# A prologue re-cut: x loaded in parts of 10, 10, 8 and 4, more filler matmuls, and one S2 group issued earlier

## The chip, the cores and the metric

The kernel runs on one core of a Trainium2 chip. The time is the device time of one execution in microseconds; smaller is better. Kernels are compared with runs of the kernel before, or of one another, on the same chip in the same rounds.

Engine names: PE is the matmul engine (PEld its weight loads), DVE the vector engine, ACT the scalar engine, POOL GpSimd, SP the queue that issues the stores. In a profile row the first two numbers are the start and the duration in us, L253 is a line of that kernel, `out<-in` are the program's tiles, xN the number of instructions merged into the row, and the bracket at the end tells how long the engine had been idle and what ended the wait. A "look" is one profiled execution. A part of x has "landed" when its transfer is complete. To "evict" is to copy a finished matmul result out of the matmul engine's output memory (PSUM). A "filler" is a matmul on zeros that nobody reads. "Cold" means that the profile shows half the full clock for PE (0.50 in its clock column; "warm": 1.00). The changed kernel has one line more near the top, so L252, L261, L277, L285, L293, L314 of the kernel before are L253, L262, L278, L286, L294, L315 of the changed one.

## The reference, cut to what matters

```python
X = np.fft.rfft(x, axis=1)                    # x: 8 x 3008 x 256
Y = X * (filt_r + 1j * filt_i)[None]
y = np.fft.irfft(Y, n=3008, axis=1).astype(np.float32)
h = y.reshape(24064, 256) @ w_in              # 256 x 2048
out = np.maximum(0.01 * h, h) @ w_out         # 2048 x 256
```

The Fourier part is done as matmuls: 3008 = 94 x 32 is split into n1 (94) and n2 (32). S1 is the transform over n1 (one matmul for each n2), a transpose on DVE (T1) turns the tile, S2 is the transform over n2, the filter is a product on DVE or POOL, SA and SB are the inverse of S2 and S1 with a transpose (T2) between. Then come the two matmuls of the MoE part with a leaky ReLU between.

## The kernel before

The first batch element cannot hide behind anything, so the kernel has a prologue of its own for it, cut into two halves of the channels (hf). All later elements run inside the slots of the MoE loop. The parts that the change touches:

```python
    for i in range(FP):                       # FP = 4, step = 8 n2
        x_load(0, step * i, step)
    ...
def first_s1(n0, n, kind, copy):              # n matmuls, then one eviction by DVE or ACT
def first_s2(hf, c, n, on_pool):              # n // 4 matmuls, products on DVE, or ACT copies and POOL
def first_sa(hf, c):                          # needs the products; evicted by ACT
def keep_warm(n):                             # n matmuls on zeros that nobody reads
    ...
    keep_warm(28)
    for g in range(6):
        first_s1(4 * g, 4, "ph", (dve, act)[g % 2])
        if g % 2:
            keep_warm(3)
    for g in range(4):
        first_s1(24 + 2 * g, 2, two[g == 3], (act, dve)[g % 2])
    keep_warm(11)
    t1_part(0, 0, True)(), t1_part(0, 1, True)()
    ...
    first_s2(1, 8, 8, True)
    first_sa(0, 8), first_sa(0, 20)
    first_s2(1, 0, 8, False)
    keep_warm(3)
    ...
    first_s2(1, 16, 8, False)
    keep_warm(4)
    first_sa(1, 0)
    keep_warm(4)
    first_t2(0), first_t2(1)
    first_sa(1, 16), first_sa(1, 8)
    first_t2(2), first_t2(3)
```

Of the kernel before, what the change touches and what calls it, by code (L numbers as in the profile page):

```python
# [18 lines left out]
N1, N2 = 94, 32  # L19
# [3 lines left out]
FP = 4  # L23
# [42 lines left out]
def kernel(  # L66
# [50 lines left out]
    def bank(kind, n, w):  # L117
        of = wide if kind == "ph" else single
        t = of[turn[kind] % len(of)]
        turn[kind] += 1  # L120
        return t[:, : n * w].rearrange("p (n w) -> p n w", n=n)
# [7 lines left out]
    def x_load(b, n0=0, nn=N2, d0=0, dn=D):  # L129

        for lo, cnt in ((0, R1),) if b + 1 < B else ((0, 64), (64, N1 - 64)):
            nc.gpsimd.dma_start(  # L132
                x_sb[lo : lo + cnt, ds(n0, nn), ds(d0, dn)],
                bass.AP(tensor=x.tensor, offset=x.offset + (b * N + lo * N2 + n0) * D + d0,
                        ap=[[N2 * D, cnt], [D, nn], [1, dn]]))
# [10 lines left out]
    step = N2 // FP  # L146
    for i in range(FP):
        nc.sync.dma_start(f1_sb[:, ts(i, step), :], f1_d.ap()[i])
    nc.sync.dma_start(small_sb[:], small_d.ap())
    for i in range(FP):  # L150
        x_load(0, step * i, step)
    for hf in range(2):
        filt_load(fa_sb, filt_r, hf * DH, DH)
        filt_load(fb_sb, filt_i, hf * DH, DH)
# [23 lines left out]
    def paired(t):  # L178
        return t[:].rearrange("p (e n t) -> p n e t", n=Q, t=2)

    def spread(dst, n0, ps, copy, e0=0):
        nn, de = ps.shape[1], ps.shape[2] // 2
        copy(paired(dst)[:, ds(n0, nn), ds(e0, de)], ps.rearrange("p n (e t) -> p n e t", t=2))  # L183
# [3 lines left out]
    def t1_part(b, i, flat=False):  # L187
        def go():
            a = big[(4 * b) % 3][:].bitcast(FP32)[:, ts(i, E4 * Q)].rearrange("p (e n) -> p e n", n=Q)
            o = big[(4 * b + 1) % 3][:].bitcast(FP32)  # L190
            if flat:
                o = o[:, ts(i, E4 * Q)].rearrange("p (e n) -> p e n", n=Q)
            else:
                o = o.rearrange("p (n e) -> p e n", n=Q)[:, ts(i, E4), :]
            nc.vector.transpose(o, a)  # L195
        return go
# [49 lines left out]
    two = ("pf", "ph")  # L246
    act, dve = nc.scalar.copy, nc.vector.tensor_copy

    def first_s1(n0, n, kind, copy):
        ps = bank(kind, n, D)  # L250
        for j in range(n):
            nc.tensor.matmul(ps[:, j, :], f1_sb[:N1, n0 + j, :], x_sb[:N1, n0 + j, :],  # L252
                             start=True, stop=True)  # L253
        spread(big[0], n0, ps, copy)


    def first_s2(hf, c, n, on_pool):
        ps = bank("ph", n, DH)
        src = paired(big[1])
        for j in range(0, n, 4):  # L260
            nc.tensor.matmul(ps[:, ds(j, 4), :].rearrange("p n (e t) -> p n e t", t=2), fwd2,  # L261
                             src[:, ds(c + j, 4), ts(hf, DH // 2)], start=True, stop=True)  # L262
        fs = [f[:, ds(c, n), ts(hf, DH)] for f in (fa_sb, fb_sb)]
        if on_pool:
            y = [outp.tile([P, n, DH], FP16, tag="ost", name=f"fy{i}_h{hf}_c{c}") for i in range(2)]
            xs = [scrp.tile([P, 4, DH], FP32, tag=f"p{j // 4 + 1}", name=f"fx_h{hf}_c{c + j}")
                  for j in range(0, n, 4)]
            for j, xf in enumerate(xs):
                act(xf[:], ps[:, ts(j, 4), :])
            for i in range(2):  # L270
                for j, xf in enumerate(xs):
                    nc.gpsimd.tensor_tensor(y[i][:, ts(j, 4), :], xf[:], fs[i][:, ts(j, 4), :], AL.mult)
        else:
            y = [ypp.tile([P, n, DH], FP16, tag=f"yw{i}", bufs=2, name=f"fy{i}_h{hf}_c{c}")
                 for i in range(2)]
            for i in range(2):
                nc.vector.tensor_tensor(y[i][:], ps, fs[i], AL.mult)  # L277
        ys[(hf, c)] = y  # L278

    def first_sa(hf, c):  # L280
        y = ys.pop((hf, c))
        for j in range(0, y[0].shape[1], 4):
            ps = bank("pf", 4, DH)
            for i, m in enumerate((inv2, inv2x)):
                nc.tensor.matmul(ps, m, y[i][:, ds(j, 4), :], start=(i == 0), stop=(i == 1))  # L285
            act(paired(big[2])[:, ds(c + j, 4), ts(hf, DH // 2)],  # L286
                ps.rearrange("p n (t e) -> p n e t", t=2))
# [24 lines left out]
    def keep_warm(n):  # L312
        for _ in range(n):
            nc.tensor.matmul(po_ps.rearrange("p a d -> p (a d)"), idle[:, 0:P], idle[:],  # L314
                             start=True, stop=True)  # L315

    keep_warm(28)
    for g in range(6):
        first_s1(4 * g, 4, "ph", (dve, act)[g % 2])
        if g % 2:  # L320
            keep_warm(3)
    for g in range(4):
        first_s1(24 + 2 * g, 2, two[g == 3], (act, dve)[g % 2])
    keep_warm(11)
    t1_part(0, 0, True)(), t1_part(0, 1, True)()
    upper(0)
    first_s2(0, 8, 8, True)
# [9 lines left out]
    first_sa(0, 0), first_sa(0, 16)  # L337
    keep_warm(3)
    first_s2(1, 8, 8, True)
    first_sa(0, 8), first_sa(0, 20)  # L340
    first_s2(1, 0, 8, False)
    keep_warm(3)
    nc.gpsimd.dma_start(w_out_sb[:], moe_w_out.rearrange("(ct p) d -> p ct d", p=P))
    first_s2(1, 16, 8, False)
# [84 lines left out]
    for slot in range(SL * (NCHUNK + 1)):  # L429
        ci, g = divmod(slot, SL)  # L430
# [36 lines left out]
```

## Time and profile before

| | value | from |
|---|---|---|
| time, median of 3 executions | 785.71 us (785.61 to 785.92) | result |
| span of the profiled one | 784.2 us (its own time was 786.34 us) | page, result |
| first S1 matmul | 9.23 us | timeline of PE |
| last part of x landed | 15.6 us | issue start plus time to landing |
| first T1 transpose | 17.70 us | timeline of DVE |
| first MoE matmul | 43.88 us | timeline of PE |
| from there to the end | 740.3 us | 784.2 - 43.88 |

A change of the prologue can only shift the start of those 740.3 us. The prediction shows the rows of PE and DVE. Here is the chain of waits of the kernel before through the second half (start, us, what):

```profile
29.40 1.07 ACT fx_h_c L269 x2
30.47 1.00 ACT big L286 x2
31.48 0.06 issue
31.53 1.48 DVE fy_h_c L277 x2
33.02 0.79 issue
33.81 2.36 DVE fy_h_c L277 x2
...
36.62 2.15 ACT big L286 x4
```

The chain runs over ACT's copies and evictions up to 31.5 us and then over DVE's products.

### The profile page before, as it was taken

To read this page: it belongs to the slowest core of one execution; us is meant where nothing else is said; L and a number is where in the kernel's file an instruction comes from. 1 tells how busy PE (TensorE), PEld (TensorE's weight loads), DVE (VectorE), ACT (ScalarE), POOL (GpSimd) and SP (SyncE) were. 2 spreads that over 40 slices of the span, in tenths; PEclk is the share of its full clock that TensorE was granted. 3 is DMA by queue.
4 is the path that set the end of the run, shared out by engine and by line. 5 is a ranking of instruction groups with operands and counts; after the bars stand their busy time and mean duration, and the time that the engine had idled before them with its cause. 6 is when DMAs were issued, how large, how long until landed. Compare 5 with 4: busy or idle time off the path is not lost.

```text
span 784.2 us, 13678 instructions
## 1 busy us (share of the span) xinstructions
PE 775.1 (99%) x5844; PEld 531.3 (68%) x5844; DVE 366.2 (47%) x458; ACT 556.0 (71%) x790; POOL 148.9 (19%) x122
## 2 busy tenths in 40 slices
PE   8999999999999999999999999999999999999998
PEld 4366677666776677766777667776677667676666
DVE  4868760874337642477306754088432765200000
ACT  3686769676686767877687776967669776666664
POOL 4863300250003300052001410024000340000000
PEclk9999999999999999999999999999999999999999
DMA  9943101401041101501104101140100101101111
GB/s 187 210 67 79 38 31 40 109 28 42 28 92 57 35 34 36 112 29 42 36 34 108 41 28 41 33 115 28 41 28 34 36 28 41 41 28 41 41 41 55
DMA packets 36252, 43.38 MB, mean 55 GB/s; under 512 B 8130, under 2 KB 34370, under 8 KB 35522
## 3 DMA queue, kind: packets, MB, share of 16 engines
q0 software_dynamic: 10000, 16.99, 12.3%
q1 hardware_dynamic: 26192, 25.53, 9.3%
q8 instruction: 45, 0.74, 0.4%
q14 instruction: 15, 0.12, 0.0%
HBM read 34.10 MB, written 24.64 MB: 75 GB/s over the span
## 4 chain that ended last, share of the span: by engine, by line
PE 92%; ACT 2%; DVE 1%; issue 1%; ACTq 0%
PE po_ps L389 41%; PE ph L375 40%; PE pf L172 3%; PE pf L239 2%; PE pf L227 2%; PE pf L212 2%; PE pf L389 1%; ACT big L183 1%; ACT gt_c L380 1%; DVE fy_h_c L277 0%; ACT big L286 0%; DVE big L293 0%; PE ph L302 0%; ACT ost_c_t L396 0%; PE pf L302 0%
## 5 line engine op out<-in xcount | busy, mean ns | idle before, releaser
L380 ACT ACTIVATE gt_c<-ph 128x1024 f16<-128x1024 f32 x376 | 385.2, 1025 | 194.5 <-PE ph L375 193.5
L375 PE MATMUL ph<-yt,w_in_sb 128*128 128x512 f16 (+7 forms) x1728 | 386.6, 351 | 0.4 <-ACT gt_c L380 0.2
L389 PE MATMUL po_ps<-w_out_sb,gt_c 128*128 128x256 f16 x2944 | 381.4, 272 | 0.6 <-ACT ost_c_t L396 0.6
L389 PEld LDWEIGHTS <-gt_c 128*128 128x128 f16 x3008 | 290.6, 98 | 86.8 <-issue 1.7
L375 PEld LDWEIGHTS <-w_in_sb 128*128 128x128 f16 x1728 | 162.9, 98 | 95.2 <-issue 1.0
L220 POOL TENSOR_TENSOR y_b_g<-p_b_g,p_b_g 128x512 f16<-128x512 f32 x84 | 107.0, 1273 | 225.8 <-DVE p_b_g L218 225.8
L195 DVE STREAM_TRANSPOSE big<-big 128x1024 f32<-128x1024 f32 x32 | 55.9, 1845 | 127.0 <-ACT big L183 126.8
L183 ACT CAST big<-pf 128x512 f16<-128x512 f32 x190 | 108.9, 606 | 0.2 <-PE pf L252 0.2
L242 DVE CAST yt<-pf 128x376 f16<-128x376 f32 x112 | 56.3, 545 | 85.9 <-PE pf L239 85.9
L216 DVE TENSOR_TENSOR p_b_g<-pf,fa_sb 128x512 f32<-128x512 f32 x84 | 58.1, 692 | 38.8 <-PE pf L212 36.3
L396 ACT COPY ost_c_t<-po_ps 128x256 f32<-128x256 f32 x184 | 69.3, 377 | 6.6 <-PE po_ps L389 5.5
L203 DVE STREAM_TRANSPOSE big<-big 128x1024 f32<-128x1024 f32 x28 | 51.1, 1932 | 34.1 <-ACT big L183 34.1
L217 DVE TENSOR_TENSOR p_b_g<-pf,fb_sb 64x512 f32<-64x512 f32 x84 | 58.2, 693 | 1.1
L218 DVE TENSOR_TENSOR p_b_g<-pf,fb_sb 64x512 f32<-64x512 f32 x84 | 57.4, 683 | 1.1
L132 POOL DMA_DIRECT2D x_sb<-in_x_dram x12 | 6.6, 555 | 255.2 <-PE pf L172 254.4
L239 PEld LDWEIGHTS <-big 128*128 128x128 f16 x448 | 25.7, 98 | 13.2
L172 PE MATMUL pf<-x_sb,f_sb 94*128 94x256 f16 x224 | 33.8, 272 | 0.1
L212 PE MATMUL pf<-big,small_sb 128*128 128x512 f16 x84 | 31.8, 379 | 0.0
L227 PE MATMUL pf<-y_b_g,small_sb 128*128 128x512 f16 x84 | 31.8, 379 | 0.0
L239 PE MATMUL pf<-i_sb,big 128*128 128x94 f16 x448 | 28.7, 206 | 0.0
L172 PEld LDWEIGHTS <-f_sb 94*128 94x128 f16 x224 | 21.0, 97 | 9.5 <-issue 1.3
L314 PE MATMUL po_ps<-idle 128*128 128x512 f16 x72 | 20.8, 432 | 1.2 <-DVE one L161 1.2
(46 smaller groups left out, 157.4 us busy)
## 6 DMA issues: line engine op xcount, KB each, us to landing
out_dram<-ost_c_t SPq DMA_DIRECT2D x92, 256.0 KB, 2.1
x_sb<-in_x_dram POOLq DMA_DIRECT2D x6, 1536.0 KB, 10.8
x_sb<-in_x_dram POOLq DMA_DIRECT2D x4, 384.0 KB, 10.4
w_in_sb<-in_moe_w_in_dram POOLq DMA_DIRECT2D x1, 1024.0 KB, 13.0
w_out_sb<-in_moe_w_out_dram POOLq DMA_DIRECT2D x1, 1024.0 KB, 10.2
x_sb<-in_x_dram POOLq DMA_DIRECT2D x1, 1024.0 KB, 8.1
f_sb<-fwd_const SPq DMA_DIRECT2D x4, 192.0 KB, 5.2
fa_sb<-in_filt_r_dram POOLq DMA_DIRECT2D x4, 192.0 KB, 12.4
```

The source lines that it names most:

```text
L172: nc.tensor.matmul(ps[:, j, :], f1_sb[:N1, n2, :], x_sb[:N1, n2, :], start=True, stop=True)
L183: copy(paired(dst)[:, ds(n0, nn), ds(e0, de)], ps.rearrange("p n (e t) -> p n e t", t=2))
L216: nc.vector.tensor_tensor(p1[:], ps, fa, AL.mult)
L217: nc.vector.tensor_tensor(p2[0:64], ps[64:P], fb[64:P], AL.mult)
L218: nc.vector.tensor_tensor(p2[64:P], ps[0:64], fb[0:64], AL.mult)
L220: nc.gpsimd.tensor_tensor(y1[:], p1[:], p2[:], AL.add)
L239: nc.tensor.matmul(ps[:, j, :], src[:, dt, n2, :], i1_sb[:, n2, :], start=True, stop=True)
L242: copy(yv[:, :, ds(4 * h, 4)], ps.rearrange("p c a -> p a c"))
L375: nc.tensor.matmul(ph[:, j, ds(o, ln)], w_in_sb[:, dt, ts(ct, P)], yts[b % 2][:, dt, ds(lo, ln)], start=(dt == 0), stop=(dt == NDT - 1),)
L380: nc.scalar.activation(gts[ci][:, ds(2 * g, 2), :], ph, AF.Lrelu)
L389: nc.tensor.matmul(po, gts[ci][:, ct, ts(tj, P)], w_out_sb[:, ct, :], start=(ct == 0), stop=(ct == NCT - 1))
L396: nc.scalar.copy(ost[:, tj % 2, :], po)
```

## The change

Its intent: less work left after the last x has landed, a warm PE when S2 begins, and no wait of DVE for the second half's first S2 group of its own.

```diff
-    for i in range(FP):
-        x_load(0, step * i, step)
+    first_parts = ((0, 10), (10, 10), (20, 8), (28, 4))
+    for n0, nn in first_parts:
+        x_load(0, n0, nn)
 ...
     keep_warm(28)
-    for g in range(6):
-        first_s1(4 * g, 4, "ph", (dve, act)[g % 2])
-        if g % 2:
-            keep_warm(3)
-    for g in range(4):
-        first_s1(24 + 2 * g, 2, two[g == 3], (act, dve)[g % 2])
-    keep_warm(11)
+    g = 0
+    for n0, nn in first_parts:
+        while nn:
+            n = 2 if nn % 4 or n0 >= N2 - 4 else 4
+            first_s1(n0, n, two[n // 4], (dve, act)[g % 2])
+            n0, nn, g = n0 + n, nn - n, g + 1
+        keep_warm(5 if n0 < N2 else 14)
 ...
     first_s2(1, 8, 8, True)
+    first_s2(1, 0, 8, False)
     first_sa(0, 8), first_sa(0, 20)
-    first_s2(1, 0, 8, False)
     keep_warm(3)
```

## The prediction

> **What bounds the kernel now.** I read the page first, then the chain of waits in order of time, then the timeline of each engine from 8.5 to 46 us, then the busy time by stretches.
>
> ```profile
> PE 775.1 (99%) x5844; PEld 531.3 (68%) x5844; DVE 366.2 (47%) x458; ACT 556.0 (71%) x790; POOL 148.9 (19%) x122
> ...
> PE 92%; ACT 2%; DVE 1%; issue 1%; ACTq 0%
> ...
> 55.00:100.00 45.00, 44.97 (x295) 28.84 (x295) 37.19 (x43) 33.45 (x47) 15.31 (x12) 1.00 0.27 65
> ```
>
> PE is busy 99% of the span, and from 55 us on it is busy without a gap (44.97 of 45.00). The change touches nothing there, so it can only move the moment at which that stretch starts: all that it wins or loses is a shift of the prologue, 44 us of 784 up to the first MoE matmul (43.88 us). The 99% also deceives in the prologue, because the fillers (matmuls on zeros) count as busy.
>
> The prologue, as DVE and PE lived it:
>
> ```profile
> 13.79 1.03 PE L252 MATMUL ph<-x_sb,f_sb 94*128 94x256 f16 x8 [0.37 <-DMA x_sb<-in_x_dram]
> 14.66 0.81 PE L314 MATMUL po_ps<-idle 128*128 128x512 f16 x3
> 15.66 0.82 PE L252 MATMUL pf<-x_sb,f_sb 94*128 94x256 f16 x6 [0.18 <-DMA x_sb<-in_x_dram]
> ...
> 16.53 2.54 PE L314 MATMUL po_ps<-idle 128*128 128x512 f16 x11
> 20.22 1.88 PE L261 MATMUL ph<-big,small_sb 128*128 128x512 f16 x4 [1.14 <-DVE big L195]
> ...
> 28.26 1.02 PE L261 MATMUL ph<-big,small_sb 128*128 128x512 f16 x2
> 29.11 1.47 PE L285 MATMUL pf<-fy_h_c,small_sb 128*128 128x512 f16 x6
> 30.42 1.02 PE L261 MATMUL ph<-big,small_sb 128*128 128x512 f16 x2
> ```
>
> ```profile
> 17.70 2.37 DVE L195 STREAM_TRANSPOSE big<-big 128x1024 f32<-128x1024 f32 x2
> ...
> 22.19 1.23 DVE L277 TENSOR_TENSOR fy_h_c<-ph,fa_sb 128x1024 f16<-128x1024 f32 x1 [1.13 <-PE ph L261]
> ...
> 28.24 1.90 DVE L309 COPY fb_sb<-fb_sb 64x3072 f16<-64x3072 f16 x1
> 31.53 1.22 DVE L277 TENSOR_TENSOR fy_h_c<-ph,fa_sb 128x1024 f16<-128x1024 f32 x1 [1.40 <-ACT big L286]
> ...
> 38.79 2.37 DVE L293 STREAM_TRANSPOSE big<-big 128x1024 f32<-128x1024 f32 x2 [0.36 <-ACT big L286]
> ```
>
> The reader should see four things. Up to 15.66 us PE waits for x, so the end of S1 is set by the last landing. From 17.70 us the path is DVE: transposes, products from 22.19 with almost no gap to 30.14, then a hole of 1.40 us. That hole is put down to ACT, but DVE's product needs the second half's S2 group, which PE begins only at 30.42, after six SA matmuls: PE's program order is the cause. Finally the last transposes (38.79) wait for ACT's evictions of the late SA groups.
>
> [...] the stretch 20.22 to 25.50 us has a mean granted clock of 0.68, which is 0.32 x 5.28 / 0.5 = 3.4 us at half speed, after the gap of 1.14 us before S2. Elsewhere the prologue stays at 0.99 to 1.00. [...] S2 reads 4-byte pairs 128 bytes apart[...]: two S2 matmuls take 1.02 us at full clock (28.26), a single one about 0.59, so 0.43 each, while SA's go at 0.22 (six in 1.47, less a tail of 0.38, over five). So S2 costs 0.43 us warm or cold, and **keeping PE warm buys S2 nothing**. [...] the copy at 28.24 takes 1.90 us beside a POOL product, the same copy at 20.10 only 0.95. I carry that delay over unchanged.
>
> **Part 1, x in parts of 10, 10, 8, 4.** Bytes are the same. From each issue's start plus its time to landing, the four parts land at 9.14, 11.64, 13.66 and 15.62 us, that is 0.31, 0.25 and 0.25 us for each n2. By interpolation (an estimate) the new parts land at 9.8, 12.65, 14.65 and 15.6 us. The intent is that only 4 matmuls and two evictions of two n2 remain after the last landing. With PE free at 15.66, the last evictions would begin 0.42 us (DVE) and 0.64 us (ACT) later, but the part before, landed at 14.65, keeps DVE to about 16.7 and ACT to 16.9; so they end near 17.45 and the transposes start at 17.5: 0.2 us early at best.
>
> **Part 2, fillers.** Groups of 3 after two parts of three become 5 after each of three parts, and 11 become 14: nine more, 0.216 us each. The order of the built instructions shows five of them between the part of 8 and the last part, before the matmuls that wait for it. PE is in order, so I add up: the part of 10 starts at 12.70; 10 matmuls at 0.109 (8 in 0.87 before the fillers start) end at 13.79; five fillers to 14.87; the part of 8 to 15.74; five fillers to 16.82. The last part has landed at 15.62, but **PE reaches it only at 16.82, 1.16 us later than before**. It is half as large, which gives most of this back: DVE evicts its first pair from 17.24 to 17.93, ACT the second from 17.46 to 18.03. The transposes start 0.11 later, as before: 18.14 instead of 17.70, +0.44. They end at 20.50. The 14 fillers run from 17.26 to 20.28, so they do not hold S2 up. [...] S2 starts at 20.58, **+0.36**. PE's gap shrinks from 1.14 to 0.3 us, so I expect no cold window. That window held mostly fillers, and the product at 25.77 followed the transpose's end (25.70) by 0.07 us, so its absence is worth less than 0.1 us.
>
> **Part 3, the S2 group ahead of SA.** The products begin at 22.55, and DVE's row of work to the last forward transpose (6.01 us from 22.19 to 28.20) follows: it ends at 28.54, and the second half's first S2 starts at 28.60. The moved group starts at 28.60 + 0.85 = 29.45 and is ready 1.04 later, at 30.49; DVE's copy, beside POOL, ends at 30.48. So the hole closes: the product moves from 31.53 to 30.55, **-0.98**. But the next group (columns 16 to 23) keeps its place: both orders run two S2 groups, six SA and three fillers before it, 3.67 us from the first S2 (28.26 to 31.93). It starts at 32.27 and is ready 1.04 later, so DVE, done with its two products at 32.83, waits until 33.36. Before, that product started at 33.81: **-0.45**. The inverse transposes start at 35.64 instead of 36.07.
>
> Then PE: four fillers and four SA matmuls and four fillers after 33.11 end at 35.71, and the late SA group gets its second product at about 35.75. ACT can evict from 36.35 instead of 36.62, **-0.27**; four evictions take 2.15, so the last transposes start at 38.52 instead of 38.79 and the first MoE matmul at 43.6. Moving SA back by 0.85 us delays ACT's evictions of it to about 30.9 to 32.5, but ACT then idles until 34.6, so this costs nothing.
>
> **Sum.** +0.36 from parts and fillers, -1.34 from the closed hole, +0.53 taken back by the next S2 group, +0.18 by PE and ACT at the last SA: -0.27. So 785.71 - 0.27 = **785.4 us**.
>
> **Rivals.** (a) The fillers do not hold the last part up, because the parts land and drain sooner than interpolated. Then the transposes start 0.2 us early instead of 0.44 late, and the end gains 0.6 more: 784.8. Against it: the fillers alone take 1.08 us after a part that ends 0.1 us before the next lands. (b) The clock is what the prologue suffers from, and a warm PE speeds S2 and the groups after it: up to 1.5 us, 784.2. For it: a window at half speed is there. Against it: S2's 0.43 us is the same at both clocks, and DVE has no gap in that window. (c) The reorder only moves the wait to ACT or PE, whose SA work ends no sooner; then only the delay of 0.36 stays: 786.1. For it: the next group and four fillers already take back most in my sum. (d) A larger first part lands later and the gap behind the first fillers cools PE: 10 S1 matmuls at double time lose up to 1 us, 786.5. Against it: a gap of 0.82 us before 11.74 did not cool it.
>
> **Range and chances.** (a) to (c) span 784.2 to 786.1; (d) and the scatter of a few tenths between runs widen the upper end: 784.0 to 786.4. Two per cent is 15.7 us, a third of the prologue, and no rival comes near it: same 0.98, faster 0.01, slower 0.01.
>
> **What would show it.** Right: PE starts the last S1 part near 16.8 with no idle before it; transposes at 18.1; S2 at 20.6, four in 1.9 us at full clock; no hole before the product at 30.55 but one of half a microsecond before 33.4; the last transposes at 38.5. Wrong: a last S1 part at 15.7 that waits for the DMA (a), S2 matmuls 0.22 apart (b), last transposes at 39 or later (c), or a granted clock under 1 between 10 and 17 us (d).

The forecast's sum came to +0.36 - 1.34 + 0.53 + 0.18 = -0.27 us, hence 785.4. A term of the sum: S2 was to start 0.08 us after the transposes' end (20.58 after 20.50) and not 0.15 as in the profile before (20.22 after 17.70 + 2.37 = 20.07), for a reason that was not shown. Without that term the +0.36 would be +0.44 and the sum about -0.19 us, 785.5 (an estimate). That a gap of 0.3 us would bring no cold window was the author's estimate.

## The result, and the profile after

The changed kernel took 785.29 us (median of 6, 783.85 to 785.59), the kernel before 785.9 us (median of 6, 785.61 to 786.03). The ratio is 0.9989 with a 95% interval of 0.9976 to 1.0002. A ratio here is the mean time of one kernel's fast runs over that of the other's of the same rounds, so it is not quite the ratio of the two medians.

The profiled execution spans 782.6 us instead of 784.2. Its first MoE matmul starts at 42.33 us, and 782.6 - 42.33 = 740.3: as before, nothing but the prologue has moved. The 1.6 us between the two spans is more than the change is worth: the profiled execution of before took 786.34 us, more than any of its six timed runs, and that of the changed kernel 784.44 us, the second fastest of its six. PE, from the first S1 matmul to S2:

```profile
9.38 0.38 PE L253 MATMUL pf<-x_sb,f_sb 94*128 94x256 f16 x2
9.60 1.03 PE L253 MATMUL ph<-x_sb,f_sb 94*128 94x256 f16 x8
10.47 1.24 PE L315 MATMUL po_ps<-idle 128*128 128x512 f16 x5
11.55 0.38 PE L253 MATMUL pf<-x_sb,f_sb 94*128 94x256 f16 x2
...
13.76 1.03 PE L253 MATMUL ph<-x_sb,f_sb 94*128 94x256 f16 x8
14.63 1.24 PE L315 MATMUL po_ps<-idle 128*128 128x512 f16 x5
15.71 0.60 PE L253 MATMUL pf<-x_sb,f_sb 94*128 94x256 f16 x4
16.15 3.19 PE L315 MATMUL po_ps<-idle 128*128 128x512 f16 x14
19.46 1.88 PE L262 MATMUL ph<-big,small_sb 128*128 128x512 f16 x4
```

No row carries an idle bracket: PE is never kept waiting between the first S1 matmul and S2. The four x parts landed at 8.4, 11.2, 13.5 and 14.8 us, so the last part lay ready for 0.9 us while five fillers ran. In the kernel before, the row at 15.66 does have a wait for the DMA. The four S2 matmuls take 1.88 us in both kernels, at full clock in both: in the profile after, the granted clock is 1.00 from 19.40 to 26.0 us; in the profile before, it is 1.00 from 20.22 to 22.10 us and falls only then (0.54 to 23.0, 0.50 to 25.0). DVE:

```profile
17.03 2.37 DVE L196 STREAM_TRANSPOSE big<-big 128x1024 f32<-128x1024 f32 x2 [0.21 <-ACT big L184]
...
29.39 1.22 DVE L278 TENSOR_TENSOR fy_h_c<-ph,fa_sb 128x1024 f16<-128x1024 f32 x1
30.53 1.21 DVE L278 TENSOR_TENSOR fy_h_c<-ph,fb_sb 128x1024 f16<-128x1024 f32 x1
32.12 1.22 DVE L278 TENSOR_TENSOR fy_h_c<-ph,fa_sb 128x1024 f16<-128x1024 f32 x1 [0.37 <-PE ph L262]
...
37.27 2.37 DVE L294 STREAM_TRANSPOSE big<-big 128x1024 f32<-128x1024 f32 x2 [0.52 <-ACT big L287]
```

The hole of 1.40 us ahead of the product is gone, and a new one of 0.37 us stands before the next product, for which PE's later S2 group is late. The chain of waits shows what took its place:

```profile
27.32 1.89 PE ph L262 x4
29.20 1.30 PE pf L286 x6
30.50 0.65 PE po_ps L315 x3
31.15 0.86 PE ph L262 x2
32.01 0.87 PE po_ps L315 x4
32.88 0.86 PE pf L286 x4
33.74 0.86 PE po_ps L315 x4
...
35.07 2.18 ACT big L287 x4
```

From 27.3 to 35.1 us the path is now PE's own program order. The rows `po_ps L315` are fillers: 0.65 + 0.87 + 0.86 = 2.38 us of work that nobody reads stand on the path that sets the end. That is not what their removal is worth: DVE ends the product that the last SA group needs at 34.47 us (33.26 + 1.21), just as PE reaches that group at 34.44.

The useful split is into two stretches: up to the first T1 transpose (T), and from T to the first MoE matmul. In the looks (before and after, then the experiments in the next section), in us:

| look | first S1 | last x landed | last S1 part starts | T | first MoE | T to MoE | span |
|---|---|---|---|---|---|---|---|
| before | 9.23 | 15.6 | 15.66 | 17.70 | 43.88 | 26.18 | 784.2 |
| c_before1 | 10.19 | 15.4 | 15.54 | 17.58 | 43.59 | 26.01 | 783.9 |
| c_before2 | 9.95 | 14.4 | 15.30 | 17.34 | 43.35 | 26.01 | 783.6 |
| after | 9.38 | 14.8 | 15.71 | 17.03 | 42.33 | 25.30 | 782.6 |
| c_after | 9.03 | 14.5 | 16.15 | 17.48 | 42.77 | 25.29 | 783.1 |
| e1_reorder | 9.93 | 14.7 | 15.28 | 17.32 | 42.70 | 25.38 | 783.0 |
| e2_parts | 8.85 | 14.6 | 15.17 | 16.49 | 42.40 | 25.91 | 782.7 |
| e3_fill | 10.08 | 15.6 | 15.95 | 17.98 | 43.98 | 26.00 | 784.3 |
| e4_parts_fill | 9.90 | 13.9 | 16.24 | 17.57 | 43.48 | 25.91 | 783.8 |
| e5_nohold | 9.46 | 15.1 | 15.14 | 16.65 | 41.94 | 25.29 | 782.3 |
| e6_front | 9.17 | 15.9 | 16.51 | 17.83 | 43.12 | 25.29 | 783.4 |
| e7_best | 8.66 | 14.8 | 14.83 | 16.36 | 41.08 | 24.72 | 781.4 |
| e7_again | 8.08 | 14.1 | 14.08 | 15.83 | 40.56 | 24.73 | 780.9 |
| e9_best8 (cold) | 9.11 | 15.5 | 16.95 | 19.93 | 45.26 | 25.33 | 785.6 |

In every row the span less the first MoE matmul's start is 740.3 us. T to MoE is the same to 0.1 us for kernels with the same code there, as long as no cold window falls into it, so it can be read from one warm look. The two looks with a cold window stand out: 26.18 against 26.00 and 26.01 (before), and 25.33 against 24.72 and 24.73 (e9, where the 14 fillers, partly at half clock, take 4.50 us instead of 3.19 and hold S2 up). T scatters by several tenths for one kernel, so one look says little about it.

### The profile page after: what moved, and what is told of

It reads as the page before. It is cut to its first block, busy times and chain, and to the rows that moved or that the text cites. A ratio compares the mean times of both kernels' runs of the same rounds, so it can differ in the third digit from the quotient of the medians.

```text
span 782.6 us, 13696 instructions
## 1 busy us (share of the span) xinstructions
PE 775.5 (99%) x5853; PEld 532.1 (68%) x5853; DVE 366.4 (47%) x458; ACT 556.1 (71%) x790; POOL 148.9 (19%) x122
## 4 chain that ended last, share of the span: by engine, by line
PE 93%; ACT 2%; DVE 1%; issue 1%; ACTq 0%
PE po_ps L390 41%; PE ph L376 41%; PE pf L173 3%; PE pf L240 2%; PE pf L213 2%; PE pf L228 2%; PE pf L390 1%; ACT big L184 1%; ACT gt_c L381 1%; PE ph L262 0%; PE pf L286 0%; DVE big L294 0%; PE po_ps L315 0%; ACT big L287 0%; PE ph L303 0%
## 5 line engine op out<-in xcount | busy, mean ns | idle before, releaser
L315 PE MATMUL po_ps<-idle 128*128 128x512 f16 x81 | 21.6, 411 | 1.2 <-DVE one L162 1.2
## 6 DMA issues: line engine op xcount, KB each, us to landing
x_sb<-in_x_dram POOLq DMA_DIRECT2D x6, 1536.0 KB, 11.2
w_in_sb<-in_moe_w_in_dram POOLq DMA_DIRECT2D x1, 1024.0 KB, 14.1
```

## The experiments

The theory: the reorder closes a hole that PE's program order makes; the extra fillers hold the last part of x up; the rest of the difference between the two profiles is chance in when x lands and when the first fillers end. The rivals: the parts of 10 load sooner, the clock is what counts, or the reorder only moves a wait.

The times below are the mean of five fast runs less the mean of the kernel before's nine in the same rounds. Their 95% intervals are about +-0.13%, or 1 us, so only the two runs of the last version are clear of noise by the time alone; for the others the intervals within the trace decide.

**e1_reorder: the reorder alone.**

```diff
-    first_sa(0, 8), first_sa(0, 20)
     first_s2(1, 0, 8, False)
+    first_sa(0, 8), first_sa(0, 20)
```

> Only the reorder (second half's S2 group of columns 0 to 7 ahead of the two late SA groups), x in four parts of 8 and the fillers of before. Theory A (the hole in DVE is PE's program order): the product of that group starts near 30.2 us instead of 31.5, the next group's near 33.0 instead of 33.8, the last transposes near 38.2 instead of 38.8, and the time falls by 0.6 us. Rival B (reorder only moves the wait to PE and ACT): the last transposes stay at 38.8 and the time stays within 0.2 us. In either case x lands as in the profile before (first matmul on x at 9.2, last part at 15.7), unless the landings differ from execution to execution.

Measured: 784.99 us median against 785.48, mean difference -0.72 us. DVE's two rows:

```profile
29.78 1.22 DVE L277 TENSOR_TENSOR fy_h_c<-ph,fa_sb 128x1024 f16<-128x1024 f32 x1
...
32.50 1.23 DVE L277 TENSOR_TENSOR fy_h_c<-ph,fa_sb 128x1024 f16<-128x1024 f32 x1 [0.36 <-PE ph L261]
```

Since T differs between the looks, count from T: the product starts 12.46 us after it (before: 31.53 - 17.70 = 13.83), the next group's product 15.18 (16.11), the last transposes 20.31 (21.09), the first MoE matmul 25.38. The two warm looks of before have 26.01 there, so the reorder is worth **0.63 us** (the mean difference agrees, but is within the noise). Theory A holds, B falls. It also settles a reading: the profile of before put the hole down to ACT's evictions of SA, and these are still there, but the hole went when PE got the S2 matmuls earlier.

**e2_parts: the parts alone.**

```diff
-            keep_warm(5 if n0 < N2 else 14)      # of the changed kernel
+            keep_warm(3 if n0 < N2 else 11)      # and the reorder undone
```

> Only the parts of 10, 10, 8 and 4, with the filler counts of before (3, 3, 3, 11) and no reorder. Theory A (the parts of 10 land early because the load itself runs sooner with them, as in the profile after: last part by 14.8 us): last S1 part near 15.1, transposes near 16.4 to 16.6, first MoE matmul about 1.2 us early, time down by 1 us. Rival B (the landing time is a matter of the execution, and the same bytes take the same time on average): parts land near 9.8, 12.65, 14.65, 15.6, transposes near 17.5, time down by 0.2 us or unchanged.

Measured: 785.48 us median, mean difference -0.48 us. The look agrees with theory A in its numbers (last S1 part 15.17, T 16.49, MoE 1.5 us early), but it was also the look with the earliest first S1 matmul of all with 28 first fillers (8.85), and the later landings (see below) do not let me call the early load a property of the parts. The time fell by less than the 1 us of theory A and is within the noise. T to MoE is 25.91, 0.1 us less than in the warm looks of the kernel before.

**e3_fill: the fillers alone.**

```diff
-            keep_warm(3)
+            keep_warm(5)
 ...
-    keep_warm(11)
+    keep_warm(14)
```

> Only the fillers (5 after each of three parts, 14 before the first S2), parts of 8, no reorder. My prediction's step (a warm PE buys S2 nothing, and no filler holds a landed part up here because parts of 8 land 2 us apart): no cold stretch between 22 and 25.5 us, four S2 matmuls still 1.9 us, transposes at 17.7, time within 0.2 us of before. Rival (the cold clock cost something in the prologue): S2 and what follows earlier by 0.5 us or more, time down by as much.

Measured: 786.46 us median, mean difference +0.78 us (interval of the ratio 0.9996 to 1.0022). No cold window appeared (clock 1.00 up to 26 us), S2 took 1.88 us, T to MoE is 26.00. The two later looks of the kernel before are warm too and have 26.01, so the fillers buy nothing there; against its cold look (26.18) a warm PE is worth 0.18 us, not the 0.5 of the rival. But T was 17.98, not 17.70, and I had expected no hold-up. The look shows why: the 28 first fillers ended only at 10.08, and from there PE ran without an idle row, three times 8 S1 matmuls and five fillers, up to 15.95, while the last part had landed at 15.6. So even with parts of 8 the extra fillers reach the path. From the first S1 matmul to T it takes 7.90 us, against 7.39 in the looks of the kernel before in which no landing holds S1 up (c_before1, c_before2): the fillers alone cost 0.51 us there.

**e4_parts_fill: parts and fillers, no reorder.** Against the changed kernel:

```diff
-    first_s2(1, 0, 8, False)
     first_sa(0, 8), first_sa(0, 20)
+    first_s2(1, 0, 8, False)
```

> Parts and fillers, no reorder. If the parts of 10 load sooner in every execution: last S1 part near 15.7, transposes near 17.0, S2 near 19.5, hole of 1.4 us in DVE kept, time down by about 0.7 us. If the early landing was a chance of one execution: last S1 part near 16.8, transposes near 18.1, time up by 0.3 us. In both the five fillers before the last part hold it up by about a microsecond after its landing.

Measured: 785.58 us median, mean difference -0.05 us. x landed early (13.9) and yet the last S1 part started at 16.24, 2.3 us after its landing. The time from the first S1 matmul to the last S1 part is 6.34 us, in the profile after 6.33: in both it is nothing but PE's own 28 S1 matmuls and 15 fillers. Neither of the two branches that I wrote down covers this: an early landing that is of no use.

**c_after: the changed kernel, without an edit, on the chip of the next three.**

> The changed kernel once more, on the chip of the next three and timed beside them. Theory A (from 1.2 us until the fillers before S2 PE is busy without a gap, so the transposes' start is the end of the 28 first fillers plus 42 matmul steps of fixed length; the last landing does not set it): the last S1 part starts 6.3 us after the first one (9.38 to 15.71 in the profile after), wherever the 28 fillers end, and at least 0.8 us after its data landed; from the first transposes to the first MoE matmul 25.3 us again; the span is 740.3 us more than the first MoE matmul's start. Rival B (landings set it): the last S1 part starts within 0.2 us of its landing.

Measured: 785.55 us median against 785.42, mean difference +0.08 us, where the first set of runs gave -0.84 (785.01 against 785.85). T to MoE was 25.29 again. The distance from first to last S1 part was 7.12 and not 6.3 us, because the second part of x landed late (a wait of 0.62 us for the DMA at 11.99). So "without a gap" is not always true; the last part was still reached 1.7 us after its landing, and rival B falls.

**e5_nohold: no fillers ahead of the last part.**

```diff
-        keep_warm(5 if n0 < N2 else 14)
+        keep_warm(14 if n0 == N2 else 0 if n0 == N2 - 4 else 5)
```

> The changed kernel without the five fillers between the part of 8 and the last part (14 before S2 kept). If those fillers hold the landed part up: the last S1 part starts 1.08 us earlier against the first S1 matmul, 5.25 us instead of 6.33, and the transposes start 0.5 us earlier at least (then the evictions of the part before bound them), the time falls by 0.5 to 0.8 us against the changed kernel. If they do not: transposes and time as in the changed kernel.

Measured: 784.19 us median, mean difference -1.00 us to before and 784.34 - 785.42 = -1.08 to c_after on the same chip. The last S1 part started at 15.14, with its landing (15.1), and T came 7.19 us after the first S1 matmul instead of 7.65 in the profile after and 8.45 in c_after. The five fillers did hold the landed part up. The last part came 5.68 us after the first S1 matmul and not the 5.25 expected, because now its landing stopped it. The gain in T between comparable looks is 0.5 us; the distance of the means contains chance as well.

**e6_front: 20 first fillers instead of 28.**

```diff
-    keep_warm(28)
+    keep_warm(20)
```

> The changed kernel with 20 fillers at the start instead of 28, all else kept. If the end of the first fillers sets when S1 starts: the first S1 matmul moves from 9.4 to 10.1 (seen so far) to the landing of the first x part, 8.0 to 8.7 us, everything after it moves by as much, the clock stays at full, and the time falls by 0.7 to 1.5 us against the changed kernel with less scatter. If the landing of x sets it: first S1 matmul and time as in the changed kernel.

Measured: 784.53 us median, mean difference -0.50 to before and -0.58 to c_after: in the right direction, less than expected and within the noise. In the look the first part landed only at 9.1, so the landing set the start (a wait of 1.90 us for the DMA) and the early end of the fillers could not show. PE was not cold after that gap: its three rows of eight S1 matmuls took 1.03 to 1.05 us (1.03 in the profile after, at full clock; 1.87 and 1.92 in e9's cold stretch, see below), and the run's mean granted clock is 1.0.

**e7_best and e7_again: a version from these findings.** Parts as in the change, 20 first fillers, 3 after the first two parts, none before the last one, and both late S2 groups ahead of the late SA groups, with 3 fillers left between SA groups of 11:

```diff
     first_s2(1, 8, 8, True)
     first_s2(1, 0, 8, False)
-    first_sa(0, 8), first_sa(0, 20)
-    keep_warm(3)
     nc.gpsimd.dma_start(w_out_sb[:], ...)
     first_s2(1, 16, 8, False)
-    keep_warm(4)
+    first_sa(0, 8), first_sa(0, 20)
+    keep_warm(1)
     first_sa(1, 0)
-    keep_warm(4)
+    keep_warm(2)
```

> A try at a better kernel: parts of 10, 10, 8 and 4; 20 first fillers; 3 fillers after the first two parts, none before the last one, 14 after it; and both late S2 groups of the second half ahead of the late SA groups, with 3 fillers between SA groups instead of 11. S1 then waits for the landings alone: transposes near 16.0 to 16.3 us. In the second half the product of columns 16 to 23 needs no wait (0.4 us hole closed), ACT's late evictions begin about 0.7 us sooner after the transposes, so 24.6 us from the first transposes to the first MoE matmul instead of 25.3. Sum: first MoE matmul near 40.8 us, time 781.9 to 783.5 us. Rival: with fewer fillers PE's clock falls and SA and SB take longer, and it ends within 0.5 us of the changed kernel.

> The better version once more, on another chip, beside the next one. First transposes near 16.4 us or where the landings put them, 24.7 us from there to the first MoE matmul, time 2 us under the kernel before.

Measured: 783.2 us against 785.42 (ratio 0.9975, interval 0.9963 to 0.9988), and on another chip 782.7 against 785.55 (0.9969, 0.9956 to 0.9981). It beats both kernels clear of noise, though the verdict at 2% is still "same". T to MoE is 24.72 and 24.73, 0.57 us less than the change (0.7 was expected); the run changes the order and the fillers there at once, so it does not tell which of the two won it. The timeline of DVE in e7_best:

```profile
29.86 1.22 DVE L278 TENSOR_TENSOR fy_h_c<-ph,fb_sb 128x1024 f16<-128x1024 f32 x1
31.00 1.22 DVE L278 TENSOR_TENSOR fy_h_c<-ph,fa_sb 128x1024 f16<-128x1024 f32 x1
32.13 1.21 DVE L278 TENSOR_TENSOR fy_h_c<-ph,fb_sb 128x1024 f16<-128x1024 f32 x1
33.26 2.36 DVE L294 STREAM_TRANSPOSE big<-big 128x1024 f32<-128x1024 f32 x2
35.97 2.37 DVE L294 STREAM_TRANSPOSE big<-big 128x1024 f32<-128x1024 f32 x2 [0.35 <-ACT big L287]
```

The products follow one another without a bracket; DVE is the path again, with a last wait of 0.35 us for ACT.

**c_before1, c_before2 and e9_best8: do the parts load sooner?** c_before1 and c_before2 are the kernel before without an edit. e9 is e7 with parts of 8, again without fillers ahead of the last part:

```diff
-    first_parts = ((0, 10), (10, 10), (20, 8), (28, 4))
+    first_parts = ((0, 8), (8, 8), (16, 8), (24, 8))
```

> The kernel before once more, for its landings. Last part of x landed at 15.6, 14.7 and 15.6 us in the three looks with parts of 8, at 13.9 to 15.9 (mean 14.8) in the seven with parts of 10, 10, 8 and 4. If the parts do not change the load (same bytes, same queue), the looks with parts of 8 spread like the others, mean near 15; if they do, they stay at 15.3 to 15.6.

> As the run before it: one more look at the landings with parts of 8, same two expectations.

> The better version with x in four parts of 8. In it S1 waits for the landings alone, so this measures what the parts are worth. Theory A (only the last part's size matters, the load is the same): after the last landing 8 matmuls and four evictions of two n2 instead of 4 and two, so the transposes start 1.9 to 2.0 us after the last landing (2.0 in the profile before) instead of 1.6 to 1.8 (e7: landed 14.76, transposes 16.36; bounded there by the evictions of the part before); time 0.2 to 0.4 us above the better version. Rival B (parts of 10 also load sooner): last landing later by 0.5 us or more on average, time 0.7 us or more above the better version.

The last part landed at 15.4, 14.4 and 15.5 us. With parts of 8 that makes six looks from 14.4 to 15.6 (mean 15.2), with 10, 10, 8 and 4 eight looks from 13.9 to 15.9 (mean 14.7). The ranges overlap, and the difference is no larger than the scatter: this stays open. The two looks of the kernel before also show that the last landing does not always set its S1: in c_before2 it came at 14.4 and PE reached the part at 15.30, because the first fillers had ended at 9.95.

e9 took 785.15 us median, its first run 787.74, the other four 784.23 to 785.28 (mean 784.7). The profiled run is the first, and it shows a cold stretch behind idle times (stretches of e9: us, then busy time of each engine, then the granted clock, the DMA share and GB/s):

```profile
9.00:12.00 3.00, 2.05 (x13) 1.26 (x13) 1.23 (x1) 1.01 (x1) 0.93 (x2) 0.84 1.07 226
12.00:16.00 4.00, 4.00 (x18) 2.43 (x16) 1.55 (x2) 1.01 (x1) 1.38 (x3) 0.50 1.50 187
16.00:20.00 4.00, 3.54 (x15) 1.84 (x14) 2.78 (x4) 2.56 (x3) 1.82 (x3) 0.50 1.82 180
```

After idle times of 1.96 and 0.84 us before its first two parts, PE ran at half clock from about 11.6 us on through the rest of S1 (0.50 from 12 to 20 us), and T came at 19.93, 4.4 us after the last landing instead of 1.6 to 1.7 us in e7. So this look cannot say what the parts are worth. The four warm runs are 1.6 us above e7_again's mean of 783.13 on the same chip: not the 0.2 to 0.4 us of theory A, and within what rival B said (0.7 or more). But e9 differs from e7 in more than the loads. The loop that sets the groups cuts its last part of 8 into 4, 2 and 2 n2, not into the four groups of two that the expectation had, so DVE evicts six of the eight n2: its last two evictions start 1.14 us apart (18.00 and 19.14), in the kernel before 0.61 (16.30 and 16.91). By these rows the cut alone costs about half a microsecond (an estimate). Without a warm profile the cause stays open. The same may happen to e7, whose fillers in front are the same; in its ten runs the mean granted clock was 0.999 or 1.0 each time.

## Why the prediction was right or wrong

**The time was right: 785.4 predicted, 785.29 measured.** Over both sets of runs the changed kernel's eleven runs have a mean of 785.19 us, the kernel before's fifteen 785.54: -0.35 us, where -0.27 was predicted, with an uncertainty as large as the difference; that the number came within 0.1 us is luck. That the change is within 2% was never in doubt; that it is worth a few tenths rests on the traces.

**The second half was right, step by step.** Counted from T, because T itself was off:

| step, us after T | predicted | profile after |
|---|---|---|
| S2 starts | 20.58 - 18.14 = 2.44 | 19.46 - 17.03 = 2.43 |
| product of the moved group | 30.55 - 18.14 = 12.41 | 29.39 - 17.03 = 12.36 |
| product of the next group, after a hole | 33.36 - 18.14 = 15.22 | 32.12 - 17.03 = 15.09 |
| last transposes | 38.52 - 18.14 = 20.38 | 37.27 - 17.03 = 20.24 |
| first MoE matmul | 43.6 - 18.14 = 25.46 | 42.33 - 17.03 = 25.30 |

The hole closed, about half a microsecond of it came back before the next group (a hole of 0.37 us), and more at the last SA group: in e1 the three steps came -1.37, -0.93 and -0.78 us earlier after T than in the kernel before, and by the table's predicted column -1.42, -0.89 and -0.71 were due (12.41 - 13.83, 15.22 - 16.11, 20.38 - 21.09). That kernel-before look is the cold one; against the warm c_before1 the three steps came -1.19, -0.74 and -0.60 us, so about 0.2 us of each was its cold window. What e1 showed beside the prediction is that the path in between is fillers and SA on PE; e7 took most of these fillers away, moved SA back and won the 0.57 us.

**The clock: right, on thinner evidence than it seemed.** All four S2 matmuls of the profile before ran ahead of its cold window. Only two single ones fall into it, at 22.97 and 25.11, and these took 0.63 and 0.62 us against 0.59 in the profile after (the next row starts 0.44 and 0.43 us after them; at full clock S2 matmuls start 0.43 apart); a filler takes 0.43 instead of 0.22 there. So S2 costs nearly the same cold, as predicted, and rival (b) falls; why an S2 matmul takes 0.43 us where one of SA takes 0.22 was not shown. The window is worth 26.18 - 26.01 = 0.17 us in that look, against less than 0.1 predicted and up to 1.5 in rival (b). As predicted, the changed kernel shows no such window: its eleven runs have a mean granted clock of 1.0 and the 20 runs of e3 to e6 with the same 14 fillers 0.999 or 1.0, while 8 of the kernel before's 27 runs in the experiments have 0.997 or 0.998 (3.4 us at half clock lower the mean by about 0.002). At 0.17 us in 8 of 27 runs that is a gain of about 0.05 us on average (an estimate). The window's length of 3.4 us that the prediction worked out is in the profile (clock 0.54 from 22.1 to 23.0 us, 0.50 to 25.5); the gap ahead of S2 was 1.14 us long. What brings a cold window on was not shown: the same gap of 1.14 us brought none in c_before1 and c_before2 (1.00 from 20 to 26 us), gaps of 1.07 and 0.92 us brought none in e7_best (1.00 from 9 to 20 us) and one of 1.90 us none in e6, while after 1.96 and 0.84 us e9 ran at 0.50.

**S1: the mechanism was right, the times were not.** The step that failed is "By interpolation (an estimate) the new parts land at 9.8, 12.65, 14.65 and 15.6 us" and the sum that starts from it, "the part of 10 starts at 12.70". The parts landed at 8.4 to 14.8, and the second one started at 11.55. So T came at 17.03 and 17.48 and not at 18.14. The hold-up is there as described (0.9 and 1.7 us between landing and start; predicted 1.2), and e5 proved it by taking the five fillers away. What I had missed is in a row of the first profile that I had in hand: the S1 matmul at 9.23 has no wait for the DMA in front, because the 28 first fillers ended at that very moment. Here it is, and below it the same two rows of c_before1:

```profile
1.20 8.13 PE L314 MATMUL po_ps<-idle 128*128 128x512 f16 x28 [1.20 <-DVE one L161]
9.23 1.03 PE L252 MATMUL ph<-x_sb,f_sb 94*128 94x256 f16 x8
...
1.20 9.16 PE L314 MATMUL po_ps<-idle 128*128 128x512 f16 x28 [1.20 <-DVE one L161]
10.19 1.04 PE L252 MATMUL ph<-x_sb,f_sb 94*128 94x256 f16 x8
```

The traces show why the fillers end at different times: the first ones start 0.43 us apart and the rest 0.22, and the slow ones number 9 in the profile before, 14 in c_before1 and 7 in c_after. (The clock column shows 1.00 for that stretch all the same, so the prediction's "Elsewhere the prologue stays at 0.99 to 1.00" misses it.) "Up to 15.66 us PE waits for x" took the coincidence of that one look for the rule. In c_before1 and c_before2 S1 began at 10.19 and 9.95, about 1.2 and 1.8 us after its data. Where no landing holds S1 up, T follows the first S1 matmul by 7.39 us in the kernel before (c_before1, c_before2, e1) and by 7.65 in the changed one (after; 7.67 in e4): **+0.26 us for parts and fillers together**, where +0.44 was predicted (the fillers alone cost 0.51 by e3, and the parts give about half back). S2 then starts 0.09 us sooner after T (2.43 instead of 2.52; 0.08 was predicted). So the sum for the change is +0.26, -0.09 and -0.63 from the reorder: about -0.45 us, as the looks themselves give (from the first S1 matmul to the first MoE matmul 32.95 us in the profile after, 33.40 in c_before1 and c_before2). With the reorder alone it is 32.77 us in e1, so where no landing holds S1 up, the new parts and fillers are a loss of 0.18 us (e4, without the reorder, gives the same: 33.58 against 33.40). The rest of the 1.6 us between the two profiles is when the first fillers ended, when x landed, and the one cold window.

**Rivals.** (a) is refuted in its cause (the fillers do hold the part up). (c) is refuted by e1. (d) did not occur in the changed kernel. e9 showed that idle time ahead of the first parts can be followed by half clock (0.50 from 12 to 20 us) and then costs more than the 1 us that I gave it (T came 4.4 us after the last landing instead of 1.6 to 1.7 in e7, about half a microsecond of it, by the estimate above, from the cut of the groups); there the cause of the idle time was fewer first fillers, not a larger first part.

**Slips.** The row of work that starts at 22.55 and lasts 6.01 us ends at 28.56, not 28.54; nothing turns on it. The text says that groups of 3 fillers stood "after two parts of three". They stood after all three. The count of nine additional fillers is right (15 - 9, and 14 - 11), and nothing was worked out from the phrase.

## What to carry to other kernels

Where engines run in program order, a filler is a cost as soon as the data behind it are there: put fillers where a wait is certain, none directly ahead of the last load's consumer (taking five away there moved T by 0.5 us in e5), and count those that appear in the chain of waits. Before taking one profile's start times as the rule, look whether a row has a wait in front of it and take a second look, then compare intervals within the trace (here from the first transpose on, repeatable to 0.1 us in warm looks) and not only times that scatter by 1 us. Moving work that the path needs ahead of work that only an idle engine needs was worth 0.63 us for two swapped lines. Carried further, and with fillers cut in both stretches, the version e7 came to 1.95 and 2.45 us under the kernel before, 1.29 us of it from the first transpose on (26.01 - 24.72).
